# Attention, output projection and mixer rebuilt from pairs of 64-row products, with GpSimd no-ops between two turns and the mixer behind attention

## The chip, the cores and the metric

The kernel runs on one core of one Trainium2 chip. The metric is device time in microseconds (us), the median of several runs. Before the change it is 821.14 us (three runs, 821.08 to 821.35).

## What is computed

2048 tokens of width 576 are normalized; the normalized `xn` goes through attention (32 query heads of 128 over the last 512 of the cached keys and values of 16 heads) and, apart from that, through a block that shifts channels along the sequence (the mixer) and then applies a feed-forward layer (the MLP). The second result gates the first. Cut to what matters:

```python
def _A_ref(x, k_cache, v_cache, wq, wo):          # D 576, Hq 32, Hkv 16, Dh 128, W 512
    q = (x @ wq) by heads
    k, v = the last W rows of the caches, each head used by two query heads
    p = softmax(q k^T * Dh ** -0.5)
    return (p v, heads side by side) @ wo
def _B_ref(x, w1, w2, w3, w4):
    h = gelu(layernorm(x) @ w1)                     # w1 576x576
    g0..g3 = the four quarters of h's columns, moved along the sequence by +1, -1, +2, -2
    x1 = x + concat(g0, g1, g2, g3) @ w2            # the mixer
    return x1 + gelu(layernorm(x1) @ w3) @ w4       # the MLP: w3 576x4608, w4 4608x576
xn = layernorm(x)
return x + _A_ref(xn, ...) * silu(_B_ref(xn, ...))
```

## The kernel before, in words

The tokens are cut into four blocks of 512. A **unit** is one head of one block, so attention has 128 units. In each unit TensorE (PE) computes the head's queries (L471: four products of 128 rows of the inner dimension, 512 columns, into `psq`), the scores of four chunks of 128 keys (L492: one 128x512 product each, into `sc`, one bank of PSUM), and, one unit later, the values (L511: 16 products of 128x129 columns, of which the 129th column sums the softmax weights, into `po`). ScalarE (ACT) takes the exponential of each score bank (L496). VectorE (DVE) inverts the sums (L515) and scales the values (L516) for two of the four query tiles at a time, out of two `po` buffers. A transposing DMA on SyncE's queue then lays the head's output out as `oT` (L524).

The inner dimension of 576 is four and a half times 128. The half is done for four heads at once (`rest_q`, L450 to L461), as two pairs of 64-row products: one works in rows 0 to 63 of the PE array, the other in rows 64 to 127, and the two run side by side. There are 31 such places. Everything else in attention, the output projection with `wo` (L535, for each block: 4 times 32 products of 128x512 into `pswo` and as many of 128x64 into `pswr`) and the mixer (products with `w1` at L593 and L603, with `w2` at L676) uses 128 rows. The gelu of the mixer is put together on DVE and ACT (L620 to L644).

The order on PE, on SyncE (SP) and on GpSimd (POOL) is the program's own. Tables of unit numbers say in which unit which part of the output projection of the block before, of the mixer and of the layernorms is put between scores and values, so that PE has products to run while ACT and DVE work. The weights `wq`, `w1`, `w2`, `wo` are loaded by POOL's DMA queue (L270, L277, L351 to L357, L347), K and V mostly too. The MLP's weights `w3` and `w4` (nine slices, L907 to L918) are loaded by SP's DMA queue after the last `oT`. K heads 4 to 15 are transposed on PE (L303).

The MLP already works in pairs of 64-row products (L964, L1001), in two turns: a bank is first filled from the lower rows, and in the second turn from the upper ones, with a small DVE instruction between (a fence, L948), because the two halves of a pair must not write one bank at the same time.

## Time and profile before

| what | value |
|---|---|
| median of 3 runs | 821.14 us |
| span of the profiled execution | 819.6 us |
| PE busy | 810.0 us, 99% |
| DVE, ACT busy | 467.2 us, 456.1 us |
| POOL busy | 96.4 us |
| attention, output projection and mixer on PE | from 9.29 to 534.85 us of the span |
| MLP | from 534.85 us to the end |

The profile is of one execution, and its span is 1.5 us shorter than the median time; that much lies outside the span. Durations of matmuls contain the time through the array: two that follow each other closely overlap, so what a matmul costs PE is the distance between two starts. Some matmul records are missing (495 of 512 score products are there), so counts in the text are those of the loops.

### The profile page before, as it was taken

The page shows a single profiled execution, that of the slowest core. Times are in us where ns is not written, and L with a number is a line of the kernel's source. Part 1 is how long each engine was busy: PE and PEld are TensorE (multiplying, and loading weights), DVE is VectorE, ACT ScalarE, POOL GpSimd, SP SyncE. Part 2 cuts the span into 40 slices and gives each one's busy share as a digit, 9 for nine tenths or more (in the row PEclk, how much of TensorE's full clock was granted, in tenths as well). Part 3 has the DMA queues.
Part 4 walks back from the last instruction along what each step waited for, and adds up shares of the span by engine and source line. Part 5 has one row for each costly group of instructions (what it writes and reads, how often), then busy time and mean ns, then how long its engine had stood idle before and what let it go on. Part 6 is the DMA issues. An engine that isn't in the chain of part 4 may idle for free. (4 is left out here: it accounts for less than half of the span.)

```text
span 819.6 us, 19524 instructions
## 1 busy us (share of the span) xinstructions
PE 810.0 (99%) x7945; PEld 469.1 (57%) x8031; DVE 467.2 (57%) x1447; ACT 456.1 (56%) x821; POOL 96.4 (12%) x164
## 2 busy tenths in 40 slices
PE   9999999999999999999999999999999999999998
PEld 6666655655564565565465655455555555555555
DVE  6878645678874357964346774044246636655413
ACT  7888853588783368994457983133332433334621
POOL 3443313010100110110001100000000000000000
PEclk9999999999999999999999999999999999999999
DMA  7998983364492144673035553994001221130101
GB/s 197 193 195 197 200 151 81 84 129 76 105 145 58 43 98 120 136 142 57 13 85 121 108 109 97 294 298 101 2 2 44 65 72 45 42 96 16 45 15 38
DMA packets 144156, 84.29 MB, mean 103 GB/s; under 512 B 110128, under 2 KB 136944, under 8 KB 144064
## 3 DMA queue, kind: packets, MB, share of 16 engines
q1 hardware_dynamic: 133408, 53.61, 32.1%
q0 software_dynamic: 9408, 28.15, 13.3%
q8 instruction: 63, 1.03, 0.5%
q10 hardware_dynamic: 1248, 1.25, 0.5%
q14 instruction: 29, 0.24, 0.1%
HBM read 49.17 MB, written 9.29 MB: 71 GB/s over the span
## 5 line engine op out<-in xcount | busy, mean ns | idle before, releaser
L496 ACT ACTIVATE pT<-sc 128x512 bf16<-128x512 f32 x512 | 285.5, 598 | 99.8 <-PE sc L492 90.4
L492 PE MATMUL sc<-qT,kT 128*128 128x512 bf16 x495 | 165.8, 379 | 0.2
L511 PEld LDWEIGHTS <-pT 128*128 128x128 bf16 x2048 | 134.3, 98 | 54.5 <-issue 11.0
L511 PE MATMUL po<-v_sb,pT 128*128 128x129 bf16 x2048 | 158.1, 220 | 0.9
L471 PE MATMUL psq<-xT_b,wq_b 128*128 128x512 bf16 x469 | 125.5, 379 | 1.9
L964 PE MATMUL ph<-xT_b,w_s 64*128 64x512 bf16 x976 | 127.3, 376 | 0.0
L1001 PE MATMUL pm<-w_s,h 64*128 64x512 bf16 x864 | 122.1, 377 | 0.0
L535 PE MATMUL pswo<-wo_sb,oT 128*128 128x512 bf16 x499 | 114.9, 379 | 0.6
L982 ACT ACTIVATE h<-ph 128x512 bf16<-128x512 f32 x67 | 39.4, 597 | 130.6 <-PE ph L964 128.4
L516 DVE TENSOR_TENSOR o<-po,ri_b 128x256 bf16<-128x256 f32 x256 | 107.9, 421 | 6.4 <-DVE ri_b L515 0.3
L1001 PEld LDWEIGHTS <-h 64*128 64x128 bf16 x1728 | 70.6, 94 | 55.4
L535 PEld LDWEIGHTS <-oT 128*128 128x128 bf16 x1024 | 65.2, 98 | 56.5
L1001 PE MATMUL pr<-w_s,h 64*128 64x64 bf16 x864 | 89.9, 189 | 0.0
L964 PEld LDWEIGHTS <-w_s 64*128 64x128 bf16 x1152 | 55.8, 94 | 48.2 <-issue 0.2
L471 PEld LDWEIGHTS <-wq_b 128*128 128x128 bf16 x506 | 49.4, 98 | 57.3 <-issue 1.0
L980 DVE COPY hx<-ph 128x512 f32<-128x512 f32 x55 | 38.1, 692 | 60.3 <-PE ph L964 60.3
L515 DVE RECIPROCAL ri_b<-po 128x2 f32<-128x2 f32 x256 | 42.2, 165 | 48.6 <-PE po L511 44.6
L492 PEld LDWEIGHTS <-kT 128*128 128x128 bf16 x512 | 46.8, 98 | 25.3 <-issue 0.2
L270 POOL DMA_DIRECT2D wq_b<-in_A_wq_dram x30 | 23.3, 776 | 303.8 <-PE sc L492 303.8
L479 DVE TENSOR_TENSOR qT<-psq,rq 128x512 bf16<-128x512 f32 x62 | 42.7, 689 | 27.0 <-ACT pT L496 20.3
L481 DVE CAST qT<-psq 128x512 bf16<-128x512 f32 x40 | 27.6, 689 | 32.9 <-PE psq L456 29.6
L982 ACT ACTIVATE h<-hx 128x512 bf16<-128x512 f32 x55 | 34.6, 630 | 6.0 <-DVE hx L980 1.7
(161 smaller groups left out, 722.7 us busy)
## 6 DMA issues: line engine op xcount, KB each, us to landing
wq_b<-in_A_wq_dram POOLq DMA_DIRECT2D x30, 512.0 KB, 5.1
wo_sb<-in_A_wo_dram POOLq DMA_DIRECT2D x8, 576.0 KB, 5.3
w_s<-in_B_w_dram SPq DMA_DIRECT2D x9, 512.0 KB, 6.8
w_s<-in_B_w_dram SPq DMA_DIRECT2D x10, 288.0 KB, 5.4
x_dram<-x SPq DMA_DIRECT2D x4, 576.0 KB, 4.1
x<-x_dram SPq DMA_DIRECT2D x4, 576.0 KB, 4.1
w_s<-in_B_w_dram SPq DMA_DIRECT2D x4, 576.0 KB, 8.3
s_b<-s_dram SPq DMA_DIRECT2D x4, 576.0 KB, 6.2
```

What stands on the lines that cost most here:

```text
L471: nc.tensor.matmul(psq[:, :], lhsT=w[:, kc, hh * Dh:(hh + 1) * Dh], rhs=xT_b[qb % 2][:, kc, :], start=(kc == 0 and not (two and hh == 1)), ...
L479: behind["qT"] = nc.vector.tensor_tensor(out=qT[:, :], in0=psq[:, :], in1=rq_t.pop(u)[:, :], op=ALU.add)
L492: nc.tensor.matmul(sc[:, :], lhsT=kT[:, g, kc * P:(kc + 1) * P], rhs=qT_t[u][:, :], start=True, stop=True)
L496: behind["exp"] = nc.scalar.activation(out=pT[:, :], in_=sc[:, :], func=ACT.Exp, scale=SCALE)
L511: nc.tensor.matmul(po[:, j, :], lhsT=pTs[kc][:, tt * P:(tt + 1) * P], rhs=v_sb[:, g, kc, 0:Dh + 1], start=(kc == 0), stop=(kc == KCH - 1))
L515: nc.vector.reciprocal(out=ri, in_=po[:, :, Dh])
L516: nc.vector.tensor_tensor(out=o[:, t0:t0 + 2, :], in0=po[:, :, 0:Dh], in1=ri.unsqueeze(2).to_broadcast([P, 2, Dh]), op=ALU.mult)
L535: nc.tensor.matmul(ps, lhsT=oT_t[qb * Hq + h][:, tt, :], rhs=wo_sb[:, h, lo:hi], start=(h == 0), stop=(h == Hq - 1))
L964: nc.tensor.matmul(ps[i][:, :], lhsT=lhsT, rhs=xT[half, kc, :], start=first, stop=last, skip_group_check=True)
L980: nc.vector.tensor_copy(out=src[:, :], in_=ps[i][:, :])
L982: nc.scalar.activation(out=h3[:, :], in_=src[:, :], func=ACT.Gelu_apprx_tanh)
L1001: nc.tensor.matmul(out, lhsT=h3_t[b, fc][half, tt * P:(tt + 1) * P], rhs=w4_s[fc // WS][half, fc % WS, lo:hi], start=key not in started, s ...
```

## The change

**Pairs.** All products of attention, the output projection and the mixer now run as pairs of 64-row products in two turns, each pair into two banks. A **fence** is a no-op in POOL's instruction stream (`nc.gpsimd.nop`, 483 of them): it waits for the last product of turn 0, and the first weight load of turn 1 waits for it.

**Queries** (`q_steps`): two heads at a time, nine pair steps: four in turn 0, four in turn 1, and a last one in which the 64-row rests of both heads make a pair. **Scores**: a `sc` tile holds two banks, so a unit has two turns for each of two tiles, and one exponential of 128x1024 elements per tile. **Values**: all four query tiles in one `po` tile of two banks, of which there is one buffer instead of two; turn 0 of unit u runs in unit u+1, turn 1 (`values_end`) in unit u+2, followed by one inversion of 128x4 and one scaling of 128x512 elements.

**Output projection** (`wo_phase`): one stretch of PE work for each block, at units 40, 72, 104 and behind the last unit, with the layernorms of the mixer's and of later blocks' input on DVE in it. **Mixer**: it runs behind attention, in an order written by hand, with one gelu on ACT for two banks; `x1` stays in memory on the chip. The transposes of K heads 4 to 15 go to SP's DMA queue, K and V loads to SP too, and the loads of `wq` are spread, one DMA per unit. The weights of mixer **and MLP** are issued by POOL, ahead of the mixer in the program.

```diff
+    def fence(*mms):
+        f = nc.gpsimd.nop(nofuse=True)
+        for m in mms:
+            sync(f, m)
+        return f
...
+        def q_steps(G):
...
+            def step(i):
...
+                if i == 2 * NF:
+                    pairs = ((c, LO, NF, j), (a, HI, NF, j))
+                elif i < NF:
+                    pairs = ((a, LO, i, 2 * j), (c, HI, i, 2 * j + 1))
+                else:
+                    pairs = ((c, LO, i - NF, 2 * j + 1), (a, HI, i - NF, 2 * j))
+                for ps, half, kc, m in pairs:
...
+                    if i == NF:
+                        sync(r, turn_t["q", G])
+                if i == NF - 1:
+                    turn_t["q", G] = fence(r)
...
-        ps_sc = pool("ps_sc", 3, PSUM)
-        ps_pq = pool("ps_pq", 2, PSUM)
-        ps_po = pool("ps_po", 2, PSUM)
-        ps_wo = pool("ps_wo", 1, PSUM)
+            ps_s = pool("ps_s", 2, PSUM)
+            ps_o = pool("ps_o", 1, PSUM)
...
+                scores(u, 0, 0)
+                for fn in load_at.get(u, ()):
+                    fn()
+                q_next(n1)
+                if u - 2 in po_t:
+                    values_end(u - 2)
+                scores(u, 0, 1)
+                exps(u, 0)
+                q_next(n - n1 - n3)
+                scores(u, 1, 0)
+                q_next(n3)
+                if n and not q:
+                    q_out(min(u // 2 + 1, GQ))
+                if u >= 1:
+                    values(u - 1, 0)
+                scores(u, 1, 1)
+                exps(u, 1)
...
+            rest(0)
+            main(0, 0)
+            rest(1)
...
+        up(0)
+        up(1)
+        shift(0)
+        up(2)
+        shift(1)
+        down(0)
+        ln3.extend(ln3_steps(0))
+        ln3_next(4)
+        up(3)
+        down(1)
+        shift(2)
+        shift(3)
+        ln3_next(5)
+        ln3_transpose(0)
+        down(2)
+        down(3)
...
+        def load_w(i):
+            c0 = i * WS * P
+            nc.gpsimd.dma_start(out=w3_s[i][:, :, :],
+                                in_=B_w3[0:NF * P, c0:c0 + WS * P].rearrange("(kc p) f -> p kc f", p=P))
...
+        for i in range(NSL):
+            load_w(i)
...
+            mixer(w1_sb, w2_sb, hb, h4, hT, hs, ps_d, ps_r)
...
-            nc.sync.dma_start(out=w3_s[i][:, :, :],
-                              in_=B_w3[0:NF * P, c0:c0 + WS * P].rearrange("(kc p) f -> p kc f", p=P))
```

**The MLP's weights before.** On SP's queue, behind the last transposes of attention (L524) and two other transfers: `w_s` and `w3r_s` are the slices of w3 and w4, and each issue waits for a semaphore of SP's eight DMA slots.

```order
187 L524 DMA_TRANSPOSE oT<-o 128x4x128 [waits DMAHW6_49,DVE_49,PE_49]
188 L200 DMA x_9071<-x_dram 128x4x576 [waits DMASW6_49,DMAHW5_49,DMASW5_49,DMAHW7_49,DMASW4_49,DMASW3_49]
189 L909 DMA w_s_8975<-in_B_w_dram 128x4x512 [waits DMAHW0_49,PE_49]
190 L913 DMA w3r_s_8976<-in_B_w_dram 64x2x128 [waits DMAHW1_49]
191 L913 DMA w3r_s_8976<-in_B_w_dram 64x2x128 [waits DMAHW2_49]
192 L916 DMA w_s_8977<-in_B_w_dram 128x4x576 [waits DMAHW3_49]
```

Now they stand in POOL's stream, behind the weights of the mixer (`h_all` holds w1 and w2 here); four issues for each of nine slices, rows 128 to 163, each waiting for the landing of the issue eight before it. Row 140 (slice 3) and row 155 (slice 6) also wait for PE.

```order
117 L903 DMA h_all<-in_B_w_dram 128x4x576
118 L905 DMA h_all<-in_B_w_dram 64x576 x2
119 L907 DMA h_all<-in_B_w_dram 128x4x576 [waits DMASW1_49]
...
128 L915 DMA w_s_11585<-in_B_w_dram 128x4x512 [waits DMASW2_49]
129 L919 DMA w3r_s_11586<-in_B_w_dram 64x2x128 [waits DMASW3_49]
130 L919 DMA w3r_s_11586<-in_B_w_dram 64x2x128 [waits DMASW4_49]
131 L920 DMA w_s_11587<-in_B_w_dram 128x4x576 [waits DMASW5_49,DVE_49]
...
140 L915 DMA w_s_11594<-in_B_w_dram 128x4x512 [waits DMAHW5_49,DMAHW3_49,DMAHW7_49,DMASW6_49,PE_49]
...
155 L920 DMA w_s_11605<-in_B_w_dram 128x4x576 [waits DMASW5_49,PE_49]
...
163 L920 DMA w_s_11611<-in_B_w_dram 128x4x576 [waits DMASW5_49]
164 L1192 TENSOR_LOAD flag_i [waits PE_49,DVE_49]
```

These rows leave no-ops out. In the built program the mixer's first no-op stands behind row 163 and ahead of row 164, the last no-op of the output projection ahead of row 113.

**The mixer's first products on PE.** Before, they stand inside attention's units (here `w1`'s products, ahead of the scores of a unit) and wait for nothing of POOL.

```order
3190 L511 MATMUL po_3257<-v_sb_90,pT_3199 128x129
3191 L593 LDWEIGHTS w1_sb_94
3192 L593 MATMUL ph_3251<-xnnT_93,w1_sb_94 128x512
...
3197 L492 LDWEIGHTS kT_89
3198 L492 MATMUL sc_3281<-qT_3153,kT_89 128x512 [waits Activation_49]
```

Now (L731 is the mixer's helper for a product) they follow the last output projection: turn 0 of the rests from row 16805, turn 0 of the first two column chunks from row 16837, and from row 16853 turn 1 of the rests. `Pool_sequencer` is the semaphore that a no-op raises.

```order
16805 L731 LDWEIGHTS xnnT_b0_90 [waits DMASW6_49,DVE_49]
16806 L731 MATMUL pr__11672<-h_all_11584,xnnT_b0_90 128x64 [waits PE_49]
...
16837 L731 LDWEIGHTS h_all_11584 [waits PE_49]
16838 L731 MATMUL pd_11670<-xnnT_b0_90,h_all_11584 128x512 [waits Activation_49]
...
16853 L731 LDWEIGHTS xnnT_b0_90 [waits Pool_sequencer_49]
16854 L731 MATMUL pr__11673<-h_all_11584,xnnT_b0_90 128x64
```

So PE's third group of products in the mixer stands behind a no-op which stands behind all of the MLP's weight issues.

**Values in a unit on PE.** Before, the two `po` tiles of a unit, eight products each, each tile waiting for DVE to have emptied the same buffer's earlier tile:

```order
5185 L492 LDWEIGHTS kT_89
5186 L492 MATMUL sc_5161<-qT_5076,kT_89 128x512 [waits Activation_49]
5187 L511 LDWEIGHTS pT_5069 [waits DVE_49]
5188 L511 MATMUL po_5164<-v_sb_90,pT_5069 128x129 [waits PE_49]
...
5203 L492 LDWEIGHTS kT_89
5204 L492 MATMUL sc_5175<-qT_5076,kT_89 128x512 [waits Activation_49]
```

Now (L408 is the helper for a product) turn 1 of the unit before last, from row 717, ends the tile `po_669`; rows 749 to 772 are turns of scores and queries; turn 0 of the last unit's values, row 773, starts `po_741` in the one buffer, and waits for DVE.

```order
713 L408 LDWEIGHTS wq_b0_99 [waits Pool_sequencer_49]
714 L408 MATMUL psq_630<-xT_b0_74,wq_b0_99 128x512
...
717 L408 LDWEIGHTS pT_583 [waits Pool_sequencer_49]
718 L408 MATMUL po_669<-v_sb_98,pT_583 128x129
...
749 L408 LDWEIGHTS kT_97 [waits Pool_sequencer_49]
750 L408 MATMUL sc_693<-qT_597,kT_97 128x512
...
773 L408 LDWEIGHTS pT_656 [waits DVE_49]
774 L408 MATMUL po_741<-v_sb_98,pT_656 128x129 [waits PE_49]
```

Between the end of one tile and the start of the next there are now the scores, queries and nothing else; the second `po` buffer is gone.

More of the change, by code (lines that the diff above doesn't have):

```diff
@@ L403, in ln1_first @@
             return mv, nb
[L405 to L406 removed]
         def x_banks():
[L409 removed]
+            pairs = [ps_x.tile([P, 2, QB], BF16, name="ps_x", tag="x") for _ in range(3)]
             return [pairs[kc // 2][:, kc % 2, :] for kc in range(NDC)]
@@ L486, in stage_s @@
[L486 to L498 removed]
+                nc.vector.tensor_reduce(out=mx[:, k, b:b + 1], in_=ri_b[:, b % 2, :, :], axis=AX.XY, op=op)
@@ L826 @@
+        for tt in range(TB):
+            add(18 + 2 * tt, lambda tt=tt: transpose_tile(xT_b[1], xn_b[1], tt))
+        order.enter_context(tc.manual_schedule(engines={SP, POOL, PE, DVE, ACTE}))
+        if True:
             mv, nb = ln1_first()
-            wu = ps_sc.tile([P, QB], FP32, name="warm", tag="sc")
+            wu = ps_warm.tile([P, QB], FP32, name="warm")
             def warm(n):
```

925 lines of the change are left out of this document (436 added, 489 removed).

## The prediction

> **What bounds the kernel now.** I read the page first, then busy time by stage, then PE's timeline, to see what one product costs.
>
> ```profile
> span 819.6 us, 19524 instructions
> PE 810.0 (99%) x7945; PEld 469.1 (57%) x8031; DVE 467.2 (57%) x1447; ACT 456.1 (56%) x821; POOL 96.4 (12%) x164
> PEclk9999999999999999999999999999999999999999
> ```
>
> PE is the bound, at the granted clock nearly everywhere. The stages (span, PE, PEld, DVE, ACT, POOL busy, clock, DMA share, GB/s):
>
> ```profile
> 0.00:9.29 9.29, 7.47 (x90) 7.40 (x91) 4.92 (x18) 4.84 (x10) 3.76 (x13) 1.00 0.81 209
> 9.29:534.85 525.57, 521.30 (x4513) 305.46 (x4592) 327.90 (x1043) 349.33 (x641) 92.61 (x151) 1.00 0.59 124
> 534.85:819.60 284.75, 281.22 (x3347) 156.19 (x3349) 134.41 (x387) 101.88 (x171) 0.00 (x0) 1.00 0.21 61
> ```
>
> The change rebuilds the middle row. What a product costs there is the distance between starts on PE's timeline:
>
> ```profile
> 64.14 0.81 PE L492 MATMUL sc<-qT,kT 128*128 128x512 bf16 x3
> 64.79 1.03 PE L471 MATMUL psq<-xT_b,wq_b 128*128 128x512 bf16 x4
> 65.75 0.39 PE L456 MATMUL psq<-xT_b,wq_b 64*128 64x512 bf16 x2
> 65.97 0.38 PE L456 MATMUL sc<-xT_b,wq_b 64*128 64x512 bf16 x2
> 66.28 0.63 PE L511 MATMUL po<-v_sb,pT 128*128 128x129 bf16 x8
> ```
>
> ```profile
> 154.35 0.62 PE L511 MATMUL po<-v_sb,pT 128*128 128x129 bf16 x8
> 154.81 1.36 PE L535 MATMUL pswr<-wo_sb,oT 128*128 128x64 bf16 x41
> ```
>
> Three score products take 0.65 us: 216 ns each. Eight value products take 0.46: 57 each. The 41 of 64 columns: (1.36 - 0.19)/40 = 29. Four query products and the change to 64 rows take 0.96, that is 864 + 96 ns, and a pair followed by the change back takes 0.31 instead of 0.22. By the loops the middle stage is 120.5 (queries) + 4.3 (first heads) + 110.6 (scores) + 116.7 (values) + 125.4 (wo) + 39.2 (mixer) + 2.7 (48 key transposes at 57) + 5.8 (31 mode changes and returns, 188 ns) = 525.2 us, against 525.6 measured. So PE waits for nothing there: a change can win only work that goes, and every new wait shows in full.
>
> **The change part by part.** *Pairs.* The MLP shows their price:
>
> ```profile
> 599.42 1.04 PE L964 MATMUL ph<-xT_b,w_s 64*128 64x512 bf16 x8
> 600.28 0.40 PE L1001 MATMUL pm<-w_s,h 64*128 64x512 bf16 x2
> 600.50 0.21 PE L1001 MATMUL pr<-w_s,h 64*128 64x64 bf16 x2
> 600.53 0.40 PE L1001 MATMUL pm<-w_s,h 64*128 64x512 bf16 x2
> ```
>
> Four pairs in 0.86 us are 216 a pair; a wide and a narrow pair take 0.25. So a pair costs what a 128-row product did: scores, values and wo stay at their price. What goes: the mode changes (5.8), the key transposes (2.7; now DMAs, issued six units, some 16 us, ahead of use), in the mixer the half chunk that was paid in full (18 pairs of each width instead of 20 products, 8 times 2 x 245 ns = 3.9), and the same for the first heads (0.4): **-12.8 us**, an ideal of 512.4 for the stage. No trace shows long rows of narrow pairs alone; between 29 ns and the two products one after the other (58) lies 0 to 3.7 us for the 128 that stand alone at the ends of the output projections. I take 0, as in the row at 600.50.
>
> *ACT.* One exponential per two banks:
>
> ```profile
> L496 ACT ACTIVATE pT<-sc 128x512 bf16<-128x512 f32 x512 | 285.5, 598 | 99.8 <-PE sc L492 90.4 <-PE ph L593 0.8
> L556 ACT ACTIVATE x<-pswr 128x256 bf16<-128x256 f32 x3 | 1.2, 384 | 1.6 <-PE pswr L535 1.5
> ```
>
> 256 columns more cost 214 ns, so 1024 take 598 + 428 = 1.03 us. Four of those and a copy of 0.6 are 4.7 us in two units, which last 5.5 on PE: ACT hides.
>
> *The single `po` buffer.* Turn 0 of unit u's values needs the tile of u-1 emptied. DVE's price:
>
> ```profile
> L516 DVE TENSOR_TENSOR o<-po,ri_b 128x256 bf16<-128x256 f32 x256 | 107.9, 421 | 6.4 <-DVE ri_b L515 0.3
> L479 DVE TENSOR_TENSOR qT<-psq,rq 128x512 bf16<-128x512 f32 x62 | 42.7, 689 | 27.0 <-ACT pT L496 20.3 <-PE psq L471 6.4
> ```
>
> ```profile
> 319.05 0.62 PE L511 MATMUL po<-v_sb,pT 128*128 128x129 bf16 x8
> 319.72 0.16 DVE L515 RECIPROCAL ri_b<-po 128x2 f32<-128x2 f32 x1
> 319.91 0.42 DVE L516 TENSOR_TENSOR o<-po,ri_b 128x256 bf16<-128x256 f32 x1
> ```
>
> ```profile
> 10.78 0.69 DVE L855 CAST qT<-psq 128x512 bf16<-128x512 f32 x1 [0.29 <-PE psq L851]
> 11.52 1.02 PE L492 MATMUL sc<-qT,kT 128*128 128x512 bf16 x4
> ```
>
> PE's eight value products that end at 319.67 let DVE start at 319.72, 0.05 later; the way back is 0.05 (the cast that ends at 11.47 and the scores behind it). From the start of turn 1 on PE: 8 pairs, 0.46; 0.18 until the last is through (220 ns a product instead of 57, and the second of a pair 19 ns late); 0.04 to DVE; inversion to scaling 0.20; scaling 0.69, the price of 512 columns; back to the weight load and the product 0.11: 1.68 us. In an odd unit the order puts five wide pairs (two of scores, three of queries) between turn 1 and the next tile's turn 0, 0.46 + 5 x 0.216 = 1.54 from turn 1's start: PE waits 0.14. In an even unit there is one pair more, and no wait. The second wait: the cast of the first query bank (0.18 + 0.04 + 0.69 + 0.05 = 0.96 behind the last pair) must end before the next pair of heads starts; a values turn and two score pairs, 0.89, lie between: 0.07. Together 0.2 us per two units, 64 times: **+12.8 us**. It is a difference of near-equal things: if DVE is 0.14 quicker most of it goes, if each wait is 0.1 longer it is near 20; the ends are 4 and 20 (none at all is rival 3).
>
> *The fences.* A no-op runs on POOL while another tile's products cover it (0.9 us or more), as long as POOL is not in a DMA issue: in attention each of those is under 0.8 us and one per unit, put behind the first fence. I take 0 there. The mixer is another matter: its first no-op stands behind all weight issues.
>
> ```profile
> L277 POOL DMA_DIRECT2D wq_b<-in_A_wq_dram x60 | 36.0, 605 | 0.0
> L270 POOL DMA_DIRECT2D wq_b<-in_A_wq_dram x30 | 23.3, 776 | 303.8 <-PE sc L492 303.8
> L347 POOL DMA_DIRECT2D wo_sb<-in_A_wo_dram x8 | 6.3, 786 | 2.3 <-issue 2.2
> L356 POOL DMA_DIRECT2D w_sb<-in_B_w_dram x4 | 2.2, 556 | 0.0
> L351 POOL DMA_DIRECT2D w_sb<-in_B_w_dram x1 | 0.8, 756 | 0.1
> ```
>
> ```profile
> 512.00:540.00 28.00, 27.89 (x263) 14.79 (x265) 1.79 (x7) 5.85 (x10) 1.87 (x3) 1.00 1.08 301
> ```
>
> POOL's last no-op of the output projection falls at its half, 15.7 us ahead of its end T (a block's projection is 128 x 0.245 = 31.4 us). From there: memsets 0.5; w1 and w2 0.76 + 0.79 + 10 x 0.556 = 7.1; nine slices of 0.776 + 2 x 0.605 + 0.786 = 2.77, 24.9. So POOL reaches the mixer's no-op at T + 16.8 at the earliest. By landings (each issue waits for that of eight before, two slices back): some 1.4 MB for w1 and w2 and seven slices of 1.18 MB are 9.7 MB, at 301 GB/s 32 us: T + 17, and 2 to 5 more for the last to land. PE has 8 x 29 + 4 x 216 = 1.1 us of mixer work in front. It then waits between 15.7 and 21: I take **+18 us**. Before, the same transfers went under attention's end on SP's queue, with no one behind them.
>
> *The clock after it.* The start of the span shows a cold array:
>
> ```profile
> 1.81 4.66 PE L831 MATMUL warm<-ident 128*128 128x112 bf16 x48 [1.81 <-POOL ident masks.py:199]
> 7.29 0.81 PE L431 MATMUL ps_k<-ident,x 128*128 128x128 bf16 x8
> 7.94 1.00 PE L415 MATMUL ps_x<-ident,xn_b 128*128 128x128 bf16 x15
> ```
>
> 48 products of 112 columns start 93 ns apart, twice what 112 columns at 216/512 cost, though the stage's row gives the clock as 1.00; the eight at 7.29 start 81 apart on the mean, the fifteen at 7.94 54. So the change is at about 7.7. From 1.81 that is 5.9 us at half speed, 2.9 us lost; for a wait of 18 us I take **+2.5** (0 to 3). The Trainium skill's TensorE: Matmul & The Clock Gate, in its table of two states, has an idle window of about 3.4 us lead to half the clock, and as long busy to leave it: an estimate from that page is 1.7 us lost. The stretch here was longer; by that figure the total would be 0.8 lower.
>
> *Waits in the mixer.* Units no longer cover it. Its three main and two rest tiles are emptied by DVE, and DVE also does the third layernorm:
>
> ```profile
> L128 DVE BATCH_NORM_STATS2 ln_st<-xn_b 128x6 f32<-128x288 bf16 x32 | 13.3, 436 | 0.0
> L129 DVE BATCH_NORM_AGGREGATE ln_mv<-ln_st 128x2 f32<-128x12 f32 x32 | 6.4, 201 | 0.2
> L139 DVE TENSOR_SCALAR xnn_b<-xn_b,ln_mv,nr_y 128x576 bf16<-128x576 bf16 x16 | 6.3, 422 | 0.1
> L176 DVE TENSOR_SCALAR xn_b<-x,ln_mv,nr_y 128x64 bf16<-128x64 bf16 x8 | 2.3, 285 | 0.0
> L113 DVE SCALAR_TENSOR_TENSOR nr_y<-nr_t,nr_y 128x4 f32<-128x4 f32 x24 | 3.9, 161 | 0.6
> ```
>
> Eleven small steps and four pairs of applies, 1.8 + 2.8 = 4.6 us, stand on DVE between `down(1)`'s adds and `down(2)`'s. `down(1)`'s adds end 1.9 us behind its products (two small ones at 0.3, one of 1024 columns at 0.69 + 2 x 0.27 = 1.2, as 256 columns more cost 0.27 above), then 4.6, then `down(2)`'s adds 1.8: the rest banks come free 8.3 us behind `down(1)`; PE wants them after `down(2)`, 18 x 0.245 = 4.4. Wait 3.7 less what overlaps, 3.5. The two other hand-overs of the rest banks wait 0.8 each, the MLP's first banks 1.9, the products behind the last gelus 1: **+8 us**, 4 to 10.
>
> *What I cost at nothing.* Layernorms in the projections: by the rows above one takes 4 x (2 x 0.44 + 0.20) + 4.6 = 8.9 us of DVE, three in one projection 27 of its 31.4; if they ran over, the next unit's scaling would be late by the excess, three times in all. The transposes of keys and the K and V loads on SP stand ahead of `oT` transposes that nobody needs before the projection. The loads of wq land a unit or more ahead of use; `x1` kept on the chip takes DMAs away that nobody waited for. The MLP's order is the same, 281 us.
>
> Sum: 819.6 + 1.5 outside the span = 821.1; 821.1 - 12.8 + 12.8 + 18 + 2.5 + 8 = **849.6 us**. With the low ends of the four waits (4, 15.7, 1, 4) it is 833.0, with the high ones (20, 21, 3, 10, and 3.7 for narrow pairs) 866.0.
>
> **Rivals.** (1) *The no-op is not held* behind the weights, as it would be if POOL's issues ran well ahead of their prices: 821.1 - 12.8 + 12.8 + 8 = 829.1 us. Against it: 36 issues at the page's durations alone outlast the projection. (2) *Narrow pairs don't run side by side*: all 656 (512 in wo, 144 in the mixer) cost 58 instead of 29, +19: 868.6 us. The pair at 600.50 speaks against it. The Trainium skill's TensorEngine Tiling (Array Packing), under Instruction Overhead, gives each matmul about 60 cycles whatever its width below that; an estimate from that is 50 ns a pair, +14 us, 863. The 29 ns of the 41 products at 154.81 fit a product's own minimum, the pair's 30 does not. (3) *The other side:* no hold and the values wait covered. Then 821.1 - 12.8 + 8 + 64 w, with w the wait per two units: faster as long as w is under 0.08 us, 816 to 819 us. DVE would have to give `po` back 0.1 us sooner than its rows say, and POOL to be through the weights when PE comes.
>
> **How the numbers follow.** Forecast 0.73, (1) 0.10, (2) 0.07, (3) 0.07, and 0.03 for a sum of waits that just eats the 12.8 us. Some 0.2% (1.6 us) is what a measurement can tell from no change. The forecast, (1) and (2) are slower: 0.90; same 0.03; faster 0.07. The range, 826 to 868, takes in the forecast's ends and (1), and leaves out (3), (2) and the 0.03 between.
>
> **What would show it.** Right: a hole of 16 to 21 us on PE at the first L731 rests with a no-op as releaser and POOL busy with L915 to L920; PE at half speed behind it; in attention a `PEld po` wait for DVE of 0.15 us in every other unit, the span from the first scores to the last projection 12 us over its share of the 512.4; mode changes gone from the waits. Wrong: a hole under 5 us there, or units of 2.75 us on average without a wait, or narrow pairs at 58 ns.

## The result, and the profile after

The changed kernel takes 864.64 us (863.41 to 865.54, 4 runs) beside 821.11 us for the kernel before (820.87 to 821.35, 4 runs): ratio 1.0529, 95% [1.0514, 1.0544]. It is 43.5 us slower. The forecast was 849.6 us with 826 to 868, so the sign and the range held, and the value was 15 us low. The profiled execution has a span of 864.0 us, 44.4 more than before. One of E6's six runs below (868.92 us) was a slow one and is left out of E6's median and ratio. The page of the changed kernel, cut to what answers to the lines shown of before:

```profile
span 864.0 us, 28244 instructions
PE 822.3 (95%) x12327; PEld 493.5 (57%) x12327; DVE 381.0 (44%) x1042; ACT 427.0 (49%) x536; POOL 101.9 (12%) x162
PEclk9999999999999999999999976989999999999999
```

PE has fallen from 99% to 95% of a longer span, and the granted clock, full in every slice before, has a dent from the 24th slice of 40 on. The busy time by stage (span, PE, PEld, DVE, ACT, POOL busy, clock, DMA share, GB/s) says how much each stage lost:

```profile
9.29:501.28 491.99, 489.81 (x8313) 307.68 (x8314) 222.17 (x587) 310.85 (x341) 82.42 (x128) 1.00 0.65 119
501.28:530.00 28.72, 3.04 (x52) 1.48 (x50) 0.23 (x1) 1.47 (x3) 18.06 (x27) 0.58 1.04 337
530.00:576.00 46.00, 38.56 (x528) 19.55 (x524) 19.17 (x50) 9.53 (x14) 0.00 (x0) 0.93 0.34 83
576.00:864.00 288.00, 283.45 (x3349) 157.78 (x3349) 134.38 (x387) 100.22 (x169) 0.00 (x0) 0.99 0.14 33
```

The first row is attention with its output projections, 14.9 us over the 477.1 that its products cost at the prices of the prediction (queries with the first heads 124.4, scores 110.6, values 116.7, projections 125.4). The second is a hole: 3 us of PE in 28.7. The third is the mixer. The fourth is the MLP with the last 0.6 us ahead of its first product, 3.3 us more than the MLP took before. The waits name the releasers (sum, count, longest):

```profile
PEld L408 <- DVE o L495: 39.3, 124, 0.6
PE pr__11673 L731 <- POOLq L193: 25.7, 1, 25.7
PE pd L731 <- DMA h_all<-h_all: 4.0, 3, 1.7
PE ph L980 <- DMA xT_b<-xnn_b: 2.5, 1, 2.5
```

The first line looks the biggest and isn't. It is the idle time of the weight load, which runs ahead of the products. What PE itself loses is read from the starts on its timeline, two units of the steady state:

```profile
440.04 0.63 PE L408 MATMUL po<-v_sb,pT 64*128 64x129 bf16 x16
...
444.00 0.65 PE L408 MATMUL po<-v_sb,pT 64*128 64x129 bf16 x15
445.32 0.47 PE L408 MATMUL psq<-xT_b,wq_b 64*128 64x512 bf16 x2
445.71 0.46 PE L408 MATMUL po<-v_sb,pT 64*128 64x129 bf16 x10
```

and on DVE between the two value turns:

```profile
444.74 0.18 DVE L494 RECIPROCAL ri_b<-po 128x4 f32<-128x4 f32 x1 [0.92 <-PE po L408]
444.96 0.69 DVE L495 TENSOR_TENSOR o<-po,ri_b 128x512 bf16<-128x512 f32 x1
```

From the start of turn 1 at 444.00 to the next tile's first product at 445.71 are 1.71 us (the prediction's sum of DVE's steps was 1.68). The last query pair starts at 445.32 and takes 0.22, so PE stands from 445.54 to 445.71: 0.17 us. The whole cycle, 440.04 to 445.71, is 5.67 where its products cost 5.50. That is 0.17 per two units, about 10.5 us in all. The remaining 4.4 of the stage lie in its first units (1.0), behind the last units, where the end of the last tile has little work beside it (2.8), and in small steps.

Of the hole, POOL's timeline tells the cause (start, duration, engine, line):

```profile
486.51 0.11 POOL L901 MEMSET h_all<- 128x8 bf16 x1 [5.59 <-PE pswo L408]
...
504.30 0.76 POOL L915 DMA_DIRECT2D w_s<-in_B_w_dram  x1 [1.27 <-DMA w_s<-in_B_w_dram]
508.94 0.76 POOL L915 DMA_DIRECT2D w_s<-in_B_w_dram  x1 [0.75 <-DMA w_s<-in_B_w_dram]
...
526.81 0.76 POOL L915 DMA_DIRECT2D w_s<-in_B_w_dram  x1 [2.64 <-issue]
528.75 0.79 POOL L920 DMA_DIRECT2D w_s<-in_B_w_dram  x1
```

POOL comes free at 486.5, when the last no-op of the output projection has run, and issues the weights of the mixer and of the MLP. The first slices follow each other as fast as POOL issues. From the one at 504.30 on they come 3.9 to 5.9 us apart and wait for landings: 1.18 MB in 4.0 us are 295 GB/s, so the transfers bound the issues. For the 2.64 us ahead of the last slice the profile names no releaser. The mixer's no-op stands behind the last issue, and PE waits for it:

```profile
501.51 1.03 PE L731 MATMUL pd<-xnnT_b,h_all 64*128 64x512 bf16 x8
528.22 0.23 PE L731 MATMUL pr__11673<-h_all,xnnT_b 64*128 64x64 bf16 x1 [25.68 <-POOLq L193]
```

The sum by PE's starts: -12.8 for the work that went, +14.9 in attention, +25.8 at the no-op (25.7 of it idle), +2.3 at half clock behind it, +13.6 in the rest of the mixer and at the MLP's start. That is 43.8 of the 44.4; the other 0.6 is spread over edges that I did not trace.

### The profile page after: what moved, and what is told of

It is laid out like the page before. It is cut to its first block, busy times and chain, and to the rows that moved or that the text cites. A ratio compares the mean times of both kernels' runs of the same rounds, so it can differ in the third digit from the quotient of the medians.

```text
span 864.0 us, 28244 instructions
## 1 busy us (share of the span) xinstructions
PE 822.3 (95%) x12327; PEld 493.5 (57%) x12327; DVE 381.0 (44%) x1042; ACT 427.0 (49%) x536; POOL 101.9 (12%) x162
## 4 chain that ended last, share of the span: by engine, by line
PE 90%; DMA 5%; DVE 1%; POOL 1%; issue 1%; ACT 1%; SPq 0%; POOLq 0%; ACTq 0%
PE psq L408 15%; PE po L408 14%; PE ph L980 14%; PE sc L408 13%; PE pswo L408 11%; PE pm L1017 11%; PE pm L1198 4%; DMA w_s<-in_B_w_dram 3%; PE pm L980 3%; PE pd L731 3%; PE pswr L408 1%; PE pr L1017 1%; DMA s_b<-s_dram 1%; DMA h_all<-in_B_w_dram 1%; ACT h_all L769 0%
## 5 line engine op out<-in xcount | busy, mean ns | idle before, releaser
L462 ACT ACTIVATE pT<-sc 128x1024 bf16<-128x1024 f32 x256 | 261.7, 1024 | 63.9 <-PE sc L408 50.3
L408 PE MATMUL psq<-xT_b,wq_b 64*128 64x512 bf16 (+1 forms) x1144 | 198.9, 376 | 0.5 <-DVE xT_b L391 0.3
L408 PE MATMUL sc<-qT,kT 64*128 64x512 bf16 x1024 | 184.0, 376 | 0.7 <-ACT pT L462 0.6
L408 PEld LDWEIGHTS <-pT 64*128 64x128 bf16 x4096 | 136.7, 94 | 62.6 <-DVE o L495 39.3
L408 PE MATMUL po<-v_sb,pT 64*128 64x129 bf16 x4096 | 163.8, 217 | 0.9 <-DVE o L495 0.3
L980 PE MATMUL ph<-xT_b,w_s 64*128 64x512 bf16 x976 | 127.8, 377 | 2.5 <-DMA xT_b<-xnn_b 2.5
L408 PE MATMUL pswo<-wo_sb,oT 64*128 64x512 bf16 x1024 | 123.4, 377 | 0.0
L1017 PE MATMUL pm<-w_s,h_all 64*128 64x512 bf16 x864 | 122.1, 377 | 0.0
L408 PEld LDWEIGHTS <-wq_b 64*128 64x128 bf16 (+1 forms) x1144 | 75.6, 94 | 47.5 <-issue 1.9
L408 PEld LDWEIGHTS <-oT 64*128 64x128 bf16 x2048 | 64.7, 94 | 59.0
L495 DVE TENSOR_TENSOR o<-po,ri_b 128x512 bf16<-128x512 f32 x128 | 88.6, 692 | 4.7 <-DVE ri_b L494 0.2
L1017 PE MATMUL pr<-w_s,h_all 64*128 64x64 bf16 x864 | 90.2, 189 | 0.0
L408 PE MATMUL pswr<-wo_sb,oT 64*128 64x64 bf16 x1024 | 72.4, 189 | 0.0
L531 ACT ACTIVATE st<-pswo 128x1024 bf16<-128x1024 f32 x8 | 8.2, 1024 | 116.6 <-PE pswo L408 93.8
L408 PEld LDWEIGHTS <-kT 64*128 64x128 bf16 x1024 | 56.8, 94 | 15.1 <-issue 3.3
## 6 DMA issues: line engine op xcount, KB each, us to landing
v_sb<-in_A_v_cache_dram SPq DMA_DIRECT2D x16, 128.0 KB, 5.0
```

What stands on the lines that cost most here:

```text
L408: return nc.tensor.matmul(out, lhsT=lhsT, rhs=rhs, start=first, stop=last, skip_group_check=True)
L462: nc.scalar.activation(out=pT[:, :, :], in_=sc_t.pop((u, c))[:, :, :], func=ACT.Exp, scale=SCALE)
L495: nc.vector.tensor_tensor(out=o[:].rearrange("p (s j) d -> p s j d", s=2), in0=po[:, :, :, 0:Dh], in1=ri.unsqueeze(3).to_broadcast([P, 2, ...
L980: nc.tensor.matmul(ps[i][:, :], lhsT=lhsT, rhs=xT[half, kc, :], start=first, stop=last, skip_group_check=True)
L1017: nc.tensor.matmul(out, lhsT=h3_t[b, fc][half, tt * P:(tt + 1) * P], rhs=w4_s[fc // WS][half, fc % WS, lo:hi], start=key not in started, s ...
```

## The experiments

The theory after the result: the hole, with the half clock behind it, comes from the place of the mixer's no-op *in POOL's order*, behind 36 weight issues; the values wait comes from the one `po` buffer. The rival for the hole: not the order but the 12 MB of weights in flight hold up whoever depends on any DMA in these 25 us. Every experiment was timed against the kernel before (820.9 to 821.0 us as medians) and is set against the changed kernel's 864.64 as well.

**E1, the mixer's fences on DVE.** POOL's stream no longer stands in PE's way in the mixer; the weights flow as they did.

```diff
+        def dve_fence(lo, hi):
+            f = small.tile([1, 1], FP32, name="mf")
+            return nc.vector.tensor_scalar(out=f[0:1, 0:1], in0=lo, scalar1=hi, scalar2=None, op0=ALU.add)
-                    cell[k] = fence(r)
+                    cell[k] = dve_fence(ps[k][0:1, 0, 0:1], ps[k][0:1, 1, 0:1])
```

> The fences of the mixer are small DVE instructions instead of GpSimd no-ops; all loads stay where they are, in the same order and on the same queue. Theory (the no-op stands in POOL's stream behind 36 weight issues): the wait of 25.8 us at the mixer's second group of products goes, and with it the 2.1 us at half speed behind it, and some 0 to 4 us come back because a DVE fence of down(2) stands behind the layernorm's 4.6 us: 837 to 841 us. Rival (PE waits there for the weights themselves, that is for the traffic of 12 MB, whoever makes the fence): 860 to 865 us, the wait stays under another releaser.

Measured: 874.54 us (869.76 to 876.59), ratio 1.0637 [1.0600, 1.0675]: some 10 us slower than with the no-ops. Of that, 7.9 us lie ahead of the first output projection in its profile, where the edit changes nothing (the table behind E10 has the stages of every run); its mixer is 2.8 us longer than the changed kernel's. The two waits that matter in it:

```profile
PEld L735 <- DVE mf L732: 27.6, 3, 19.6
ACT h_all L782 <- DMA h_all<-h_all: 20.4, 1, 20.4
```

and ten microseconds of its busy time (columns as above):

```profile
530.00:540.00 10.00, 0.00 (x0) 0.00 (x0) 0.00 (x0) 0.26 (x2) 2.60 (x4) 0.50 0.85 154
```

The hole has moved and not gone. A fence on DVE stands there behind a copy that waits for ACT's gelu (L782), and the gelu waits 20.4 us until the transposing DMA that still reads the buffer it overwrites is done. This DMA shares the engines with the burst of weights: the mixer's transposes took up to 20.0 us from issue to landing, 5.1 at most in the changed kernel. SP could issue them only from 522.2 on, because the load ahead of them waited until 521.5 for a store that ACT had issued at 510.5.

**E2, six of the nine slices issued behind the mixer.** The no-op keeps its engine but has 12 slice issues ahead of it and not 36.

```diff
-        for i in range(NSL):
+        for i in range(3):
             load_w(i)
...
             mixer(w1_sb, w2_sb, hb, h4, hT, hs, ps_d, ps_r)
+        for i in range(3, NSL):
+            load_w(i)
```

> Slices 3 to 8 of the MLP's weights are issued by POOL behind the mixer's last no-op instead of ahead of its first; slices 0 to 2 stay. Theory: the wait at the start of the mixer falls from 25.8 us to under 2, the clock stays up, and slice 3 lands long before the MLP reads it (a slice every 4 us, wanted every 4.3): 836 to 839 us. Rival (the traffic, not the order): the hole goes too, but moves to the MLP's products, 850 us or more. This kernel against the one with DVE fences: the same time within 4 us if both only take the no-op out from behind the issues.

Measured: 866.67 us (865.39 to 869.82), ratio 1.0569 [1.0547, 1.0591], 2.0 us over the changed kernel. The hole at the mixer's start is gone, PE goes on from 501 us. In its place stands this:

```profile
PE ph L982 <- DMA xT_b<-xnn_b: 19.8, 1, 19.8
```

```profile
560.00:570.00 10.00, 0.00 (x0) 0.00 (x0) 0.00 (x0) 0.00 (x0) 4.66 (x7) 0.50 1.35 131
```

The MLP's first product waits 19.8 us for the transposes of the third layernorm's result. SP issued them from 545.3 on, into the burst of slices 3 to 8 that POOL began at 543.9, and they took up to 24.7 us to land. In the changed kernel, without that burst, they took 2.6 and the same wait is 2.5. The shift DMAs are caught too: PE waits 10.3 us for them, 4.0 in the changed kernel. So with E1 and E2 my theory falls as the only cause: the no-op's place in POOL's order decides *who* waits, while that someone waits some 20 us comes from the burst. Whichever DMA-dependent step comes first takes it.

**E5, the remaining slices held back until the transposes have landed.** E2, and four one-element copies on POOL that read the four transposed tiles, ahead of slices 3 to 8. No burst lies under the mixer, and none under the transposes.

```diff
+        landed = small.tile([1, TB], BF16, name="landed", bufs=1)
+        for tt in range(TB):
+            nc.gpsimd.tensor_copy(out=landed[:, tt:tt + 1], in_=xT_b[0][0:1, 0, tt * P:tt * P + 1])
+        for i in range(3, NSL):
+            load_w(i)
```

> Slices 3 to 8 of the MLP's weights are issued behind the mixer and behind four small GpSimd copies that read the third layernorm's transposed output, so not before those transposes have landed; slices 0 to 2 stay ahead of the mixer. Theory (formed from the two kernels before: the weights keep the DMA engines full for some 25 us past the projection, and the mixer's own small DMAs, or the no-op, or the transposes, whichever comes first, wait behind them): no burst lies under the mixer, no hole at its start, none at the MLP's first product: 864.6 - 25.8 - 2.1 = 836.7, 836 to 840 us. Rival (the MLP needs the weights at once, so the wait only moves on): a hole of over 10 us at slice 3 in the MLP, 850 us or more.

Measured: 848.80 us (842.0 to 851.5), ratio 1.0311 [1.0265, 1.0358]: 15.8 us off the changed kernel, the hole and the half clock at the mixer's start gone. By the stages of the profile (table behind E10) the mixer is 21.9 us shorter, and the MLP, which now gets its slices later, is as long as it was. That confirms the burst. It is less than the 28.1 us of hole and clock, and the waits say where the rest lies:

```profile
PE pd L731 <- DMA h_all<-h_all: 6.2, 4, 2.5
PE ph L985 <- DMA xT_b<-xnn_b: 3.8, 1, 3.8
PE psq L408 <- DMA xT_b<-xn_b: 2.4, 1, 2.4
PE sc L408 <- DMA kT<-st: 2.2, 1, 2.2
```

The shift DMAs in the mixer cost 6.2 and the transposes 3.8, 3.5 more than in the changed kernel; why was not tested. And waits for the second block's input and for the transposed keys are new, 4.6 us in the first 102 us, where the edit changes nothing. With the clock that falls behind them, attention is 7.8 us longer up to its first output projection, and as long as before from there on.

**E4, the values wait doubled.** The reciprocal of the tile is taken twice, 0.2 us more on DVE's path; the result is the same.

```diff
-            nc.vector.reciprocal(out=ri, in_=po[:, :, :, Dh])
+            for _ in range(2):
+                nc.vector.reciprocal(out=ri, in_=po[:, :, :, Dh])
```

> The inversion of the softmax sums is done twice, which puts 0.20 us more into the way from the last value product to the free po buffer. Theory: odd units wait 0.20 more, even units (0.07 in hand) 0.13: 0.33 us per two units, 62 times, 20 us: 885 us. Rival (the wait is not on this way, or hidden by more than reckoned): 864 to 870.

Measured: 879.77 us (879.0 to 880.4), ratio 1.0714 [1.0696, 1.0732]: 15.1 over the changed kernel. On PE two units take 5.91 (from 303.99 to 309.90), so the wait is 0.41 and not 0.17; 0.24 times 62 is 15. It has two parts now. In the odd unit the last query pair starts at 303.46 and the next tile at 303.99, 0.31 later than the pair takes; in the even unit two pairs start at 300.51 and the tile at 301.04, 0.10 late. So DVE's way from turn 1 to the next tile, which was on the path in every second unit, is now on it in each. The 20 that I expected had 0.20 more for the odd unit and 0.13 for the even one; they were 0.14 and 0.10.

**E3, `po` copied out first.** One copy of 128x516 frees the bank, and DVE inverts and scales from the copy.

```diff
-            po = po_t.pop(u)[:, :, 0:2 * n].rearrange("p j (s n) -> p s j n", s=2)
+            pc = pc_pool.tile([P, 2, 2 * n], FP32, name="pc")
+            nc.vector.tensor_copy(out=pc[:], in_=po_t.pop(u)[:, :, 0:2 * n])
+            po = pc[:].rearrange("p j (s n) -> p s j n", s=2)
```

> The values are copied out of PSUM first and inverted and scaled from the copy, so the one po buffer is free again 0.20 us sooner; DVE does 128 copies of 0.69 us more. Theory (po comes back 0.15 us too late in odd units): that wait goes, the cast of the queries' first bank still costs some 0.09 per two units: 5 to 6 us of the 10.9 are won, 859 us. If the whole 0.17 goes, 854. Rival (fences or query steps make the wait): 864 or, with DVE busier, above.

Measured: 872.42 us (870.3 to 873.7), ratio 1.0621 [1.0602, 1.0640], 7.8 over the changed kernel. On its timeline of DVE:

```profile
303.94 0.69 DVE L498 TENSOR_TENSOR o<-pc,ri_b 128x512 bf16<-128x512 f32 x1
304.55 0.68 DVE L445 CAST qT<-psq 128x512 bf16<-128x512 f32 x1
```

The wait at `po` went, but scaling takes as long from the copy, 0.69, and the cast of the query bank stands behind it. PE now waits 0.29 per two units where it had waited 0.17, and 0.23 of it stand behind that cast. A wait taken from one bank went to the next one in DVE's order.

**E6, the end of the values ahead of the queries.** In each unit turn 1 of the older values and what DVE does behind it start before the query products, so that these cover DVE.

```diff
-                q_next(n1)
                 if u - 2 in po_t:
                     values_end(u - 2)
+                q_next(n1)
```

> One line is moved in attention: turn 1 of the values of the unit before last runs ahead of the unit's first query step instead of behind it. DVE gets one query pair (0.216 us) more to empty the po buffer, and the cast of the query bank 0.46 more. Theory (the wait of 0.17 us in two units is DVE's way back to po and to the query bank): both go, 864.6 - 10.9 = 853.7 us. Rival (the no-op behind the values' turn 0, which now has two wide pairs, 0.43 us, to run under, makes PE wait in each unit): 0.1 to 0.2 per unit, 860 to 870.

Measured: 856.66 us as the median of five runs, with a wide spread (853.2 to 865.2), ratio 1.0412 [1.0393, 1.0431]. The steady state is clean; its values on PE, two units apart:

```profile
429.97 0.63 PE L408 MATMUL po<-v_sb,pT 64*128 64x129 bf16 x16
...
435.46 0.63 PE L408 MATMUL po<-v_sb,pT 64*128 64x129 bf16 x16
```

5.49 us, the products' own cost. So the values wait is wholly a matter of order: the same buffer and the same DVE work cost nothing when enough products lie between. The gain of 8.0 on the medians is less than the 10.5 of that wait. Its profile, a long run of 865.2 us, shows both sides: from the first output projection to the mixer it is 7.5 us shorter, what 0.17 makes in the 44 pairs of units there, and ahead of that projection it is 7.3 us longer. The waits name what came there:

```profile
PE sc L408 <- DMA kT<-st: 5.3, 3, 2.3
PE psq L408 <- DMA xT_b<-xn_b: 3.8, 1, 3.8
```

Both lie before 102 us, where SP transposes keys and the second block's input while wq, wo and the K and V loads are in flight. The rival, PE waiting at the no-ops, does not show: the weight load stands at most 0.2 us at one, hidden behind the products.

**E7, E5 with the shifts spread out.** Half of block 2's shift DMAs go ahead of `up(3)` and half ahead of `down(1)`, where the changed kernel issues all eight behind it, and the 1.18 MB of `load_sx(0)` is issued only after the third layernorm's last transpose.

```diff
         down(0)
+        shift(2, (0, 2))
...
         up(3)
+        shift(2, (1, 3))
         down(1)
-        shift(2)
         shift(3)
...
-        load_sx(0)
+        with tc.issue_after(last_tr[0].ins):
+            load_sx(0)
```

> As the kernel with the gate; besides, half of the shift DMAs of block 2 are issued before up(3) instead of behind down(1), and the loads of the attention output and of x for the MLP's end go behind the layernorm's transposes on SP's queue. Theory (down(2) and down(3) wait for SP, which issues a shift DMA every 0.62 us, and for 1.2 MB of other loads in the same queue): 3.8 us of waits and the half-speed stretch behind them, 0.9 us, go down to about 1: 3 to 4 us under the kernel with the gate, 833 us. Rival (they wait for DVE's layernorm): no gain.

Measured: 842.86 us (835.4 to 844.5), ratio 1.0236 [1.0188, 1.0285], 5.9 off E5; in the profiles its mixer is 6.8 us shorter than E5's. The wait for `h_all` fell to 3.3; a wait of 4.7 for the second block's `xT_b` stands at the first 102 us in its profile.

**E8, E7 and E6 together.**

> The three edits together: gate, shifts and loads, values' turn 1 first. If they are independent, the gains add: 864.6 - 27.9 - 3.5 - 10.9 = 822 us, which is the kernel before within 0.3%. Rival (the waits cover each other): 828 or more.

Measured: 833.01 us (831.7 to 835.1), ratio 1.0155 [1.0138, 1.0172]: 31.6 off the changed kernel, where E7 and E6 alone give 21.8 and 8.0. Its units behind the first projection are as short as E6's and its mixer as short as E7's, so the gains add where the edits act. The 822 that I had added up did not come; the kernel is still 1.5% slower than before. What PE waits for in its profile:

```profile
PE sc L409 <- DMA kT<-st: 3.5, 3, 1.7
PE ph L987 <- DMA xT_b<-xnn_b: 3.6, 1, 3.6
PE psq L409 <- DMA xT_b<-xn_b: 3.0, 1, 3.0
```

**E9, the keys earlier.** E8 with the key transposes three units earlier, the loads of K with them, and the wo loads later.

```diff
-            add(2 * g - 6, lambda g=g: transpose_k(g))
+            add(max(2 * g - 9, 0), lambda g=g: transpose_k(g))
...
-            load(8 + 4 * i, lambda i=i: load_wo(i))
+            load(24 + 2 * i, lambda i=i: load_wo(i))
```

> The kernel with all three edits, and in attention the transposing DMAs of key heads 4 to 15 are issued three units (8 us) sooner, the loads of K for it two and three units sooner, and the eight loads of wo later (units 24 to 38 instead of 8 to 36). Theory (PE waits 8 us in all between 60 and 102 us, in the profiled run of the kernel with all three edits, for key transposes and wq loads that land late while the DMA engines are full): most of that goes, 833 - 6 = 827 us, and the runs lie closer together. Rival (they are late for another reason, such as SP's order): 832 to 834.

Measured: 832.37 us (824.2 to 834.8, six runs), ratio 1.0124 [1.0089, 1.0158]. In its profile no wait for keys is left, but the one for the transposes of the second block's input (`xT_b<-xn_b`) has grown from 3.0 to 5.7 us.

The medians show no gain over E8: inconclusive.

**E10, E9 with the mixer's shifts half a step earlier and `down` beginning with its wide pairs.**

```diff
         up(0)
+        shift(0, (0, 2))
         up(1)
-        shift(0)
+        shift(0, (1, 3))
+        shift(1, (0, 2))
...
-            for s in range(2):
-                for c in range(4):
-                    rest(s, 0, c)
-                    main(s, 0, c)
+            for c in range(4):
+                main(0, 0, c)
+            for c in range(4):
+                rest(0, 0, c)
+            for c in range(4):
+                rest(1, 0, c)
+                main(1, 0, c)
```

> As the one before, and in the mixer all shift DMAs that need no later block are issued one step sooner, and down starts with its four wide pairs instead of narrow and wide in turn, so the rest banks are wanted 0.86 us later. Theory (down(0) waits 1.7 us for its shifts, each down 0.5 to 0.7 for the rest banks): 1.7 + 3 x 0.5 = 3.2 us less than the kernel before it. Rival (SP's 0.62 us per shift DMA is the limit, whatever the order): no more than 1.5 us.

Measured: 834.22 us (830.4 to 840.4, six runs), ratio 1.0177 [1.0149, 1.0205]. Its profiled span is 828.8, E9's 831.1, but it is 4.1 shorter ahead of the first projection, where the edit changes nothing; the mixer is 0.3 us shorter and not 3.2. The medians say +1.9 the other way, inside the spread of either. Inconclusive too.

No version beats the kernel before. The best median, 832.37, is 1.2% behind it by the ratio.

**The stages of every profile.** Read from the starts on PE's timeline: from the span's start to the first product of the first output projection, from there to the mixer's first product, on to the MLP's first product, and to the end of the span (us).

| profile | to the first projection | to the mixer | mixer | MLP to the end | span |
|---|---|---|---|---|---|
| changed kernel | 128.5 | 372.8 | 75.3 | 287.4 | 864.0 |
| E1 | 136.4 | 372.8 | 78.1 | 286.5 | 873.9 |
| E2 | 128.0 | 372.8 | 75.1 | 287.9 | 863.8 |
| E3 | 132.1 | 377.6 | 73.4 | 287.7 | 870.9 |
| E4 | 132.9 | 383.6 | 74.3 | 287.8 | 878.6 |
| E5 | 136.3 | 372.8 | 53.4 | 287.4 | 849.8 |
| E6 | 135.8 | 365.3 | 74.7 | 287.7 | 863.6 |
| E7 | 135.9 | 372.8 | 46.6 | 287.7 | 842.9 |
| E8 | 132.5 | 365.3 | 46.5 | 285.8 | 830.2 |
| E9 | 131.9 | 365.3 | 48.0 | 285.9 | 831.1 |
| E10 | 127.8 | 365.3 | 47.7 | 288.0 | 828.8 |

Behind the first projection a stage differs from the changed kernel's by more than 2 us only where an edit acts. The first column does not keep to that: the changed kernel, E1, E2, E5 and E7 have the same attention, and take 128.0 to 136.4 us for the same work. In E1 the last transposes of the second block's input land at 99.9 us and PE waits 4.7 for them, in the changed kernel they land at 94.2 and it does not wait. So a total of one of these kernels can be 8 us off for a reason that its edit has nothing to do with.

## Why the prediction was right or wrong

The three terms that were well off were all too low (8 us at the no-op, 5.6 in the mixer, 2 in attention's waits); nothing cancelled, and they make up the 15 us.

- **The work that goes, -12.8: right.** The output projections run at their products' price without loss, and the mode changes are gone from the waits. Rival (2) falls: narrow pairs keep their 29 ns in rows of their own too. Two starts from the mixer's first group:

```profile
501.43 0.19 PE L731 MATMUL pr__11672<-h_all,xnnT_b 64*128 64x64 bf16 x1
501.46 0.19 PE L731 MATMUL pr__11672<-h_all,xnnT_b 64*128 64x64 bf16 x1
```

- **The exponentials hide: right.** The group's row has 1024 ns where I had worked out 1.03 us, and PE waits 0.6 us for ACT over the whole of attention.

```profile
L462 ACT ACTIVATE pT<-sc 128x1024 bf16<-128x1024 f32 x256 | 261.7, 1024 | 63.9 <-PE sc L408 50.3
```

- **The single `po` buffer, +12.8: right, 10.5 measured** in the steady state, 14.9 with the stage's ends. The step-by-step path of 1.68 us was 1.71. My second wait, 0.07 at the query bank, does not show. E4 and E6 show the mechanism from both sides; rival (3) needed a wait under 0.08 us and there were 0.17. (My high end was reckoned wrong: 0.1 more in each of two waits is 0.4 per two units and 26 us in 64, not 20.)

- **The hold at the first no-op, +18 with 21 as its high end: the mechanism is right, the size failed, 25.7.** The step that failed is "By landings": it let 9.7 MB flow at 301 GB/s from POOL's start on. POOL's start, 486.5, is what I forecast (T is 501.3). From there to the last slice's first issue:

```profile
486.50:526.81 40.31, 16.04 (x274) 8.21 (x270) 0.00 (x0) 2.49 (x4) 28.66 (x48) 0.74 0.90 284
```

  In these 40.3 us some 11.5 MB moved, at 284 GB/s on the mean. Until 501.28 it was 190 GB/s: POOL needs 7.6 us (487.10 to 494.69) to issue the 1.4 MB of w1 and w2, and only then begins the slices. From 501.28 on the row of the second stage has 337 GB/s, more than I had reckoned with, but 1.2 MB of the sum are no weights: a store of the attention output and a load of x, 0.59 MB each. By my own 301 GB/s the slow start is worth 5.5 us and the other transfers 3.9 (estimates from these rows). And the hold ends 1.4 us behind that issue, at 528.22.

- **Rival (1), 829.1 without the hold: its price was wrong.** It let all of the hold vanish with the no-op's place. E1 and E2 free the no-op and come out at 874.54 and 866.67; only where the burst itself goes, E5, do 15.8 us come back, 21.9 in the mixer.

- **The clock, +2.5: 2.3 measured.** PE runs at half speed from 528.22 to 532.9. (The low end of my sum has 1 for this term, where I had given 0 to 3; with 0 it is 832.0 and not 833.0.)

- **The mixer, +8 with 4 to 10: too low, 13.6, and only partly for the reason given.** By PE's starts, DVE's hand-overs of the rest banks and the gelus cost 2.9, and waits for the shift DMAs, which I had not priced, 4.8 (4.0 of it idle). SP's own queue shows why (issue, duration, count):

```profile
554.51 7.34 SPq L794 DMA_DIRECT2D h_all<-h_all  x8
561.90 1.14 SPq L944 DMA_DIRECT2D s_b<-s_dram  x2
563.13 6.46 SPq L794 DMA_DIRECT2D h_all<-h_all  x8
569.69 5.20 SPq L206 DMA_TRANSPOSE xT_b<-xnn_b  x4
```

  A block's eight shifts take SP 6.5 to 7.3 us. Some 0.62 us each is the issuing; in the first row SP also waits 2.4 us for the next block's transposes, in the third it is held before its last shift, which goes out at 569.08, when the load of `s_b` has landed. The transposes stand behind that one, at 569.69: the MLP's first product starts 3.0 late. The holes that these make cost more clock, 2.9.

  The third layernorm's wait of 3.5 is there too, but hidden: PE starts `down(3)` 2.6 us late, and DVE releases it,

```profile
565.09 0.19 PE L731 MATMUL pr__12341<-h_all 64*128 64x64 bf16 x1 [0.20 <-DVE xn_b L845]
```

  while PE had spent 2.0 of the 2.6 on shift DMAs just before. (By its own terms the sum had 8.3 less 4.4, which is 3.9 and not 3.7.) Before the change, units of attention lay over all of it. I had asked which engine empties the banks and not which queue feeds the products.

- **The transposes of keys at nothing: right in this kernel, by luck.** The changed kernel has no such wait; its second block's last input transposes land at 94.2 us, just in time. In the profiles of E1, E5 and E7, with the same attention, PE waits 4.6 to 5.2 us there for `kT` and `xT_b`; with the shorter units of E6 and E8 it waits 9.1 and 6.5. E9 moves the keys and finds the next transposes in the queue.

What stays open: the kernels of the experiments with the gate or the earlier end of values differ by 3 to 16 us from run to run, where the kernel before differs by less than 1. The table puts such differences ahead of the first projection, but it has one profile of each kernel. That the same waits make the spread between runs was only argued, since no kernel took all of those transposes off SP's queue, and what makes them land early or late is not known. In the profiles E5 brings back 14 us less than hole and clock had cost: 7.8 lie in that first stretch, 3.5 in longer waits for shifts and transposes in the mixer; the rest was not traced. No kernel put the burst back on SP's queue or under attention's end, where it stood before, so it is not shown that it could be hidden there with the new order.

## What to carry to other kernels

When a relay for semaphores shares a queue with DMA issues, price the queue up to its last *landing*, and then ask who else needs any DMA while that burst runs: moving the relay only chooses the next to wait (E1, E2), holding back the burst is what pays (E5). Before two pieces of work that cover each other are put one behind the other, list every queue of the second one, small transfers and transposes included. And a buffer taken away can cost nothing or 10 us depending on the order alone (E6 against the change): count the products between the last read and the next write.

## What the runs showed of the hardware

- **The clock halves, and comes back, in steps of 3.41 us.** Busy time and granted clock (the column ahead of the last two) of the changed kernel, first in the single microseconds in which the clock switched:

```profile
505.00:506.00 1.00, 0.00 (x0) 0.00 (x0) 0.00 (x0) 0.00 (x0) 0.90 (x3) 0.80 0.98 341
532.00:533.00 1.00, 1.00 (x8) 0.34 (x6) 0.00 (x0) 0.12 (x1) 0.00 (x0) 0.55 0.94 354
570.00:571.00 1.00, 0.37 (x2) 0.09 (x4) 0.00 (x0) 0.00 (x0) 0.00 (x0) 0.72 0.12 28
573.00:574.00 1.00, 1.00 (x8) 0.47 (x4) 0.25 (x2) 0.00 (x0) 0.00 (x0) 0.57 0.50 98
577.00:578.00 1.00, 1.00 (x8) 0.43 (x6) 0.00 (x0) 0.00 (x0) 0.00 (x0) 0.64 0.00 0
580.00:581.00 1.00, 1.00 (x8) 0.45 (x6) 0.21 (x1) 0.00 (x0) 0.00 (x0) 0.66 0.00 0
```

  A mean of 0.80 over 505 to 506 puts the fall to half at 505.6. In the same way the other rows give a return at 532.9, a fall at 570.44, a return at 573.86, a fall at 577.28 and a return at 580.68. These lie 8, 11, 1, 1 and 1 times 3.41 us apart, and in the traces of E1 to E10 too the switches of one trace lie whole steps apart (E8's has none). What PE did in three such steps:

```profile
560.21:563.62 3.41, 1.70 (x26) 0.93 (x24) 3.18 (x15) 0.00 (x0) 0.00 (x0) 1.00 0.22 34
567.04:570.45 3.41, 1.66 (x19) 0.62 (x15) 0.00 (x0) 0.00 (x0) 0.00 (x0) 1.00 0.16 40
573.86:577.28 3.42, 0.89 (x10) 0.41 (x10) 1.51 (x3) 0.00 (x0) 0.00 (x0) 1.00 0.41 78
```

  The second and the third ended in a fall, as did the one ahead of 505.6 with 0.36 us of work; the first did not, with a stall of 1.7 us in it. So in this trace a fall came where PE had worked less than about half of a step (an estimate from four of them), and it can come late: at 577.28 PE had already been back at work for 0.7 us. The way back took 4.7 us from 528.22 and 3.4 the other two times. The Trainium skill's TensorE: Matmul & The Clock Gate has, in its table of the two states, about 3.4 us for either way. The step is as long, and the way back agrees in two cases out of three; but 3.4 us without any work were not needed for a fall here, so a stall of 2 us can already cost its clock.

- **POOL's rows of DMA issues do not say when the next no-op runs.** PE resumes at 528.22, while POOL's row of the last slice's L920, behind which the no-op stands, is from 528.75 to 529.54. So the no-op did not wait for the end of that row, nor for its start; how the two overlap the profile does not show.

- **Small transfers are slow to issue and slower in a crowd.** SP issues one shift of 16x512 per 0.62 us where nothing holds it, and a shift lands 1.7 us after its issue at best; those issued beside the load of `s_b` in the rows above took up to 6.1. In E2's row from 560 to 570 the engines moved 131 GB/s at a busy share of 1.35, against 337 GB/s at 1.04 in the changed kernel's hole: where transposes and weights run together, busy engines are no measure of bytes moved.
